# A written-out issue order replaced by another one, with separate PSUM tiles for four early transposes and four of the last stores moved to ScalarE's queue

## The chip, the cores and the metric

The kernel runs on one NeuronCore of one Trainium2 chip. The core has five engines with instruction streams of their own: TensorE (PE in the profile; its weight loads are listed apart as PEld), VectorE (DVE), ScalarE (ACT), GpSimd (POOL, nearly unused here) and SyncE (SP), which here issues nearly all DMA transfers. The engines wait for one another through semaphores only. The metric is device time in microseconds (us); three runs of the kernel before the change took 268.01, 268.32 and 269.27 us, median 268.32 us.

## The reference

Two branches work on a layer-normed input `xn` of 2048 rows and 640 columns, and their sum is added to the raw input.

```python
xn = _layernorm(x, axis=-1)
return x + _A_ref(xn, A_k, A_v, ...) + _B_ref(xn, B_w_gate, B_w_up, B_w_down)

def _A_ref(q, k, v, shift_k, ssm_k, ssm_D):
    k_shift = k_shift + k_pad[:, t:t + S, :] * shift_k[:, ks - 1 - t][None, None, :]   # 4 taps
    kv = k_shift * v
    y = ...                       # long convolution of kv with ssm_k, by FFT of length 2 S
    return q * (y + kv * ssm_D[None, None, :])

def _B_ref(x, w_gate, w_up, w_down):
    h = _sigmoid(g) * u           # g = x @ w_gate, u = x @ w_up, 640 -> 1728
    return h @ w_down             # 1728 -> 640
```

Inputs and output are bf16, S is 2048, D is 640.

## The kernel before, in words

**Branch B** takes the 2048 rows in four row tiles (`tr`) of 512. A row tile is normalized, transposed into `xnT` (for `tr` 0 and 1 by TensorE against an identity, L707; for 2 and 3 by a transposing DMA, L701), multiplied with gate and up weights for 14 column blocks `fc` of 128 (L773: five matmuls of 128x512 to a group; for the first two blocks of `tr` 0 in four column quarters, L753), passed through a sigmoid on ScalarE (L727, L732, L738) and a product on VectorE (L729, L735, L740) into `hT`, and multiplied with `w_down` (L789: groups of 7 or 14 matmuls of 128x320). VectorE adds the result to `acc` (L801), which began as the raw input and ends as the output.

**Branch A** replaces the FFT by two rounds of small DFT matmuls over ten channel slices `idx`. For a slice, VectorE builds `kvt` (L472 to L490); stage 1 (L510) is two groups of 32 matmuls on a quarter of the array's rows; stage 2 (L530) is four groups of 32 matmuls of 64x64; VectorE multiplies the spectra (L554 to L569), which for most slices needs a copy with swapped halves that SyncE issues as two transfers (`P<-S`, L550); stage 3 (L582) is two groups of eight matmuls. After five slices, half the channels are complete, and stage 4 (L614) runs over them: 16 groups in the whole kernel, each of 64 matmuls on 32x32 tiles of the array. ScalarE, and VectorE for the numbers in `ON_DVE`, move each group's result from PSUM to SBUF (L316, L317, L319).

**What orders the work.** Each step calls `plan.op`, which gives it a number and records what it reads and writes. `ORDER` is a written-out permutation of the 984 numbers, and `emit` issues the steps in exactly that order; each engine gets its own steps as a stream and runs them in that order. A planner's due times (`pri`) and costs stand in the source, but the order no longer depends on them. `emit` also hands out buffers: of the free slots of a tag, an unused one, else the one that was used longest ago. PSUM has three slots of tag `c` (2x512 f32 to a partition) and two of tag `g` (512 f32).

The first transposes (`rec_tp` with `fast`) share `psT` tiles, two transposes in one tile of tag `c`; the seven and twelve matmuls that only warm up TensorE (L819) write a tile of tag `g`. The last stores (L632) are 24 DMA issues, all on SyncE's queue.

Of the kernel before, what the change touches and what calls it, by code (L numbers as in the profile page):

```python
# [42 lines left out]
def _dft_tables():  # L43
# [34 lines left out]


ORDER = [  # L80
    1, 0, 4, 5, 42, 6, 7, 8, 71, 12, 13, 11, 72, 10, 73, 74, 75, 91, 96, 86, 87, 76, 77, 78, 14, 2, 104, 16, 81, 625,
    79, 80, 92, 98, 97, 148, 15, 626, 43, 88, 82, 83, 643, 84, 99, 85, 17, 64, 20, 93, 607, 89, 90, 94, 100, 149, 102,
    645, 101, 644, 150, 103, 627, 629, 631, 633, 628, 632, 630, 603, 634, 605, 599, 601, 604, 61, 62, 63, 600, 606,
    602, 18, 639, 641, 650, 640, 651, 153, 152, 652, 108, 642, 635, 608, 609, 23, 637, 611, 66, 106, 67, 151, 610,
    636, 612, 155, 65, 154, 68, 19, 638, 107, 156, 58, 56, 105, 613, 44, 615, 614, 616, 57, 60, 59, 25, 157, 617, 115,
    158, 109, 646, 619, 648, 24, 618, 116, 621, 620, 647, 113, 623, 111, 622, 110, 112, 649, 120, 675, 27, 26, 624,
    122, 3, 679, 676, 117, 121, 119, 118, 123, 130, 678, 680, 22, 683, 21, 661, 124, 114, 673, 29, 662, 665, 674, 663,
    677, 133, 135, 653, 654, 664, 134, 128, 28, 159, 136, 161, 45, 666, 667, 129, 30, 125, 655, 668, 656, 126, 671,
    669, 659, 670, 660, 31, 32, 33, 35, 681, 672, 657, 34, 38, 658, 162, 682, 163, 712, 165, 181, 36, 684, 164, 166,
    37, 127, 714, 713, 703, 182, 715, 704, 705, 39, 685, 167, 168, 172, 160, 706, 298, 687, 689, 47, 171, 169, 691,  # L90
    686, 51, 302, 688, 694, 170, 131, 40, 696, 178, 180, 300, 690, 303, 692, 179, 41, 173, 695, 304, 301, 716, 183,
    195, 697, 299, 718, 196, 174, 730, 199, 49, 200, 175, 693, 201, 732, 202, 197, 176, 717, 186, 69, 177, 95, 719,
    198, 731, 185, 733, 184, 192, 720, 194, 707, 193, 698, 709, 187, 772, 53, 132, 227, 228, 189, 700, 708, 54, 233,
    231, 188, 710, 234, 721, 711, 190, 699, 191, 52, 50, 723, 138, 48, 722, 701, 743, 724, 70, 218, 55, 702, 232, 734,
    139, 744, 137, 203, 736, 213, 229, 725, 745, 46, 214, 140, 735, 727, 205, 207, 204, 206, 141, 209, 737, 230, 208,
    726, 728, 216, 210, 217, 739, 738, 219, 729, 220, 741, 143, 211, 740, 771, 212, 221, 215, 767, 742, 222, 142, 224,
    226, 223, 768, 792, 770, 252, 225, 761, 254, 285, 253, 263, 287, 144, 755, 746, 235, 237, 762, 756, 764, 264, 286,
    269, 255, 758, 270, 265, 256, 267, 239, 236, 266, 791, 241, 786, 238, 240, 257, 268, 242, 249, 773, 288, 788, 753,
    251, 775, 407, 243, 260, 261, 759, 250, 754, 245, 244, 757, 760, 146, 246, 258, 763, 289, 765, 259, 247, 766, 769,
    262, 271, 248, 273, 412, 747, 318, 272, 274, 276, 305, 748, 324, 751, 319, 320, 275, 322, 408, 290, 325, 323, 749,  # L100
    787, 750, 315, 321, 291, 145, 294, 279, 789, 277, 278, 292, 293, 280, 752, 306, 774, 297, 326, 797, 307, 327, 776,
    317, 308, 790, 799, 281, 283, 310, 284, 309, 798, 311, 295, 782, 316, 312, 296, 800, 282, 328, 147, 354, 355, 783,
    313, 784, 329, 358, 359, 331, 356, 801, 410, 360, 793, 361, 785, 777, 345, 340, 330, 314, 795, 344, 779, 414, 778,
    342, 780, 794, 343, 796, 341, 357, 781, 806, 811, 808, 334, 351, 411, 812, 332, 353, 807, 826, 335, 809, 333, 802,
    828, 352, 346, 810, 362, 348, 804, 404, 363, 803, 336, 827, 347, 349, 805, 350, 406, 365, 405, 338, 337, 829, 830,
    817, 831, 339, 926, 413, 822, 819, 424, 383, 824, 364, 367, 427, 832, 927, 418, 426, 425, 834, 818, 833, 428, 366,
    368, 369, 370, 429, 928, 820, 821, 433, 417, 430, 431, 836, 835, 371, 838, 374, 416, 432, 837, 434, 372, 454, 823,
    375, 409, 376, 463, 419, 825, 373, 377, 420, 839, 435, 840, 378, 813, 464, 379, 866, 380, 815, 384, 415, 385, 421,
    387, 814, 449, 386, 422, 423, 450, 816, 848, 850, 381, 452, 460, 851, 451, 436, 438, 388, 461, 382, 462, 437, 849,
    853, 852, 389, 453, 455, 467, 468, 469, 439, 470, 440, 841, 465, 466, 862, 441, 854, 443, 444, 390, 391, 392, 394,  # L110
    457, 863, 865, 442, 397, 398, 399, 400, 855, 456, 867, 844, 471, 401, 858, 445, 845, 458, 856, 446, 490, 459, 488,
    393, 847, 447, 448, 472, 474, 857, 485, 859, 499, 487, 877, 842, 486, 879, 476, 496, 489, 881, 479, 491, 395, 497,
    498, 843, 501, 492, 500, 493, 846, 503, 480, 505, 504, 473, 475, 477, 478, 860, 483, 883, 878, 880, 861, 502, 506,
    481, 872, 507, 484, 521, 864, 482, 494, 527, 402, 874, 523, 495, 528, 873, 882, 508, 875, 907, 509, 511, 522, 531,
    884, 532, 533, 529, 513, 510, 868, 929, 906, 512, 885, 876, 530, 870, 515, 534, 524, 931, 869, 525, 514, 517, 516,
    871, 535, 536, 930, 519, 518, 571, 933, 520, 887, 932, 921, 526, 549, 934, 550, 935, 537, 912, 551, 538, 923, 539,
    914, 541, 886, 553, 552, 555, 540, 585, 542, 554, 543, 922, 544, 924, 556, 913, 915, 925, 916, 557, 558, 917, 919,
    545, 546, 888, 918, 547, 890, 920, 889, 592, 891, 560, 562, 565, 897, 899, 901, 898, 903, 902, 559, 900, 561, 892,
    563, 566, 564, 904, 908, 905, 569, 548, 567, 894, 570, 578, 910, 893, 895, 909, 568, 586, 587, 896, 936, 589, 588,
    911, 396, 590, 591, 967, 579, 580, 582, 581, 938, 572, 573, 583, 939, 584, 575, 593, 574, 941, 576, 594, 937, 595,  # L120
    964, 577, 962, 963, 944, 960, 596, 940, 597, 942, 945, 598, 943, 947, 946, 403, 968, 9, 948, 969, 971, 950, 966,
    949, 952, 951, 970, 961, 953, 974, 972, 973, 965, 954, 975, 955, 958, 978, 977, 979, 976, 956, 957, 959, 982, 980,
    983, 981
]
ON_DVE = [
    101, 103, 135, 134, 136, 656, 660, 526, 915, 546, 548, 570, 895, 588, 581
]


# [90 lines left out]
def kernel(  # L220
# [71 lines left out]
    def make(b, tag, i):  # L292
        shape, dt = SHAPE[tag]
        if b.startswith("pst"):
            shape, dt = [P, NC, P], BF16
        if b.startswith("psT"):
            shape, dt = [P, 2, 1024], BF16
        if b == "wv":
            shape, dt = [P, 4, NC, 512], BF16
        if b in ("xk", "xv"):  # L300
            shape, dt = [P, 2, 2, 4 * DM // 2], BF16
        pool = ps if tag in ("c", "g") else wk
        return pool.tile(shape, dt, name=f"{tag}{i}", tag=f"{tag}{i}")
# [324 lines left out]
    def store(m0, m1, pri, d0=0, d1=DM):  # L628
        key = [("acc", m, x) for m in range(m0, m1) for x in range(4)] if d1 - d0 == DM else (
            [("fin", m, d0 // 320) for m in range(m0, m1)] + [("cv", m // 4) for m in range(m0, m1)])  # L630
        for q in range(4):
            dma(lambda e, q=q: e.dma_start(oq4[q][:, m0:m1, d0:d1], acc[32 * q:32 * q + 32, m0:m1, d0:d1]), 32,  # L632
                2 * (d1 - d0) * (m1 - m0), r=key, w=[("out", m0, d0, q)], pri=pri)

    MEAN, VAR, RST, TMP, EPS = range(5)

# [60 lines left out]
    def rec_tp(tr, pri, fast=False):  # L697
# [8 lines left out]
            for c5 in range(NC):  # L706
                nc.tensor.transpose(o[:, c5, :], tl[N][:, i, c5 * P:(c5 + 1) * P], ident[:])  # L707
        for i in range(4):
            p_ = f"pst{tr}_{i}" if not fast else f"psT{tr}_{i // 2}"
            o = (lambda p_=p_: tl[p_]) if not fast else (  # L710
                lambda p_=p_, i=i: tl[p_][:, i % 2, 0:NC * P].rearrange("p (c n) -> p c n", n=P))
            al = [] if fast and i % 2 else [(p_, "c" if fast else "g")]
            pe(5 * mm(128), 5, lambda i=i, o=o: tp(i, o()), r=[(N, i), ("ident",)] + ([(X, "a")] if i else []),
               w=[(p_, i)] + ([] if i else [(X, "a")]), alloc=al + ([] if i else [(X, "xnT")]), pri=FIX if fast else gt())
            ev(640, lambda i=i: tl[X][:, :, i * P:(i + 1) * P], lambda o=o: o(),
               r=[(p_, i)], w=[(X, i)], pri=pri if fast else pri - 1000)
# [99 lines left out]

    def warm(n):
        for _ in range(n):
            nc.tensor.matmul(tl["wps"][:], lhsT=tl["warm"][:, 0:P], rhs=tl["warm"][:], start=True, stop=True)  # L819
    plan.op({"PE": (4.4, lambda: warm(12))}, r=[("warm",)], w=[("wps", 0)], alloc=[("wps", "g")], pri=FIX)  # L820
    for q in range(2):
        load_x(q, 0, 1, "SP", FIX)
        load_x(q + 2, 0, 1, "ACT", FIX)
# [107 lines left out]
```

## Time and profile before

| what | value |
|---|---|
| median of the runs | 268.32 us |
| time of the profiled execution | 267.2 us |
| span, first to last instruction, of that execution | 265.4 us |
| time around the span | 1.8 us |
| mean granted TensorE clock | 0.983 |
| matmuls, weight loads | 4231, 4231 |
| DVE idle in 78 to 160 us, in 160 to 200 us, in 200 to 236 us | 2.2, 8.2, 5.2 us |

The page lists, for each group of instructions, its line, engine and shapes, its count, the time it was busy, the mean of one, and after the bar the idle time of the engine just before these instructions and what ended it ("issue" where no wait shows). The chain of waits follows the end of the program back to what released each step; a row there has start, duration, engine, tile and line.

### The profile page before, as it was taken

Reading aid. Unit: us, or ns where it says so; the run is one execution under the profiler, and the core shown is the slowest. Engines: PE = TensorE matmul, PEld = TensorE weight load, DVE = VectorE, ACT = ScalarE, POOL = GpSimd, SP = SyncE. Lnnn points to the kernel's source line nnn. Section 1 sums busy time; section 2 is a strip of 40 time slices with the busy share of each in tenths; the row PEclk is TensorE's granted clock in tenths of the full one; section 3 lists DMA queues with packets and bytes.
Section 4 is the critical chain, followed back from the end, with each engine's and each line's share of the span. In section 5 each row is a group of like instructions: output and inputs, shape, how many; then the busy total and the mean of one; then the engine's idle time right before and its main releaser. Section 6 shows DMA issues by size and latency. Waiting matters only on the chain.

```text
span 265.4 us, 9461 instructions
## 1 busy us (share of the span) xinstructions
PE 243.8 (92%) x4231; PEld 145.9 (55%) x4231; DVE 201.2 (76%) x336; ACT 177.2 (67%) x261; POOL 0.7 (0%) x6
## 2 busy tenths in 40 slices
PE   7699999899999999999999994997999899996792
PEld 3554546574455567675645562675675465454571
DVE  4522425568999999999999994896989697996640
ACT  3614699885888998967999993652799774332400
POOL 1000000000000000000000000000000000000000
PEclk9999999999999999999999998897999999999998
DMA  6999979999797199999997953663006496202652
GB/s 175 327 278 244 272 176 132 147 169 149 166 233 207 27 294 183 114 133 135 192 241 194 204 119 94 103 201 82 4 2 180 129 307 158 66 2 54 151 127 73
DMA packets 91024, 41.44 MB, mean 156 GB/s; under 512 B 66656, under 2 KB 88104, under 8 KB 90664
## 3 DMA queue, kind: packets, MB, share of 16 engines
q1 hardware_dynamic: 90792, 40.52, 70.4%
q8 instruction: 33, 0.54, 0.9%
q10 hardware_dynamic: 192, 0.33, 0.4%
q14 instruction: 7, 0.06, 0.1%
HBM read 30.61 MB, written 5.24 MB: 135 GB/s over the span
## 4 chain that ended last, share of the span: by engine, by line
PE 66%; DVE 18%; ACT 6%; issue 6%; DMA 1%; ACTq 0%; DVEq 0%
PE g L773 34%; PE g L789 15%; PE c L530 6%; PE c L614 4%; DVE P L560 3%; PE c L582 3%; ACT jk L654 2%; DVE kvt L490 2%; ACT jk L648 2%; DVE ta L477 2%; PE c L510 2%; DVE acc L801 2%; DVE S L563 1%; PE c L753 1%; DMA acc<-in_A_q_dram 1%
## 5 line engine op out<-in xcount | busy, mean ns | idle before, releaser
L773 PE MATMUL g<-xnT,w 128*128 128x512 bf16 x380 | 90.8, 383 | 0.2 <-DVE acc L801 0.2
L789 PE MATMUL g<-wd,hT 128*128 128x320 bf16 x448 | 68.0, 304 | 0.2
L773 PEld LDWEIGHTS <-w 128*128 128x128 bf16 x380 | 35.0, 98 | 38.1 <-issue 1.7
L789 PEld LDWEIGHTS <-hT 128*128 128x128 bf16 x448 | 42.8, 99 | 18.3 <-issue 0.3
L316 ACT CAST S<-c 128x1024 bf16<-128x1024 f32 x40 | 40.0, 1029 | 6.8 <-PE c L530 6.7
L740 DVE TENSOR_TENSOR hT<-sig,g 128x512 bf16<-128x512 bf16 x32 | 22.0, 686 | 26.7 <-PE g L773 25.6
L738 ACT ACTIVATE sig<-g 128x512 bf16<-128x512 f32 x32 | 19.3, 602 | 22.5 <-PE g L773 19.4
L773 PE MATMUL g<-xnT,V 128*128 128x512 bf16 x140 | 32.7, 379 | 0.1
L801 DVE TENSOR_TENSOR acc<-g,acc 128x320 bf16<-128x320 f32 x32 | 15.5, 488 | 17.8 <-PE g L789 17.7
L530 PEld LDWEIGHTS <-Mt 64*128 64x128 f16 x1280 | 20.0, 95 | 8.3 <-issue 8.0
L530 PE MATMUL c<-T,Mt 64*128 64x64 bf16 x1280 | 22.7, 190 | 1.8 <-issue 1.8
L319 ACT ACTIVATE T<-c 128x1024 bf16<-128x1024 f32 x20 | 20.2, 1028 | 2.1 <-PE c L510 2.1
L490 DVE TENSOR_TENSOR kvt<-ta,vt 128x1024 bf16<-128x1024 bf16 x10 | 21.4, 2144 | 0.1
L773 PEld LDWEIGHTS <-V 128*128 128x128 bf16 x140 | 13.2, 98 | 15.1 <-issue 0.4
L316 ACT CAST V<-c 128x1024 bf16<-128x1024 f32 x17 | 17.3, 1021 | 5.2 <-PE c L582 5.0
L316 ACT CAST T<-c 128x1024 bf16<-128x1024 f32 x19 | 18.9, 1029 | 1.4 <-PE c L510 1.4
L614 PE MATMUL c<-V,Bt 32*32 32x80 bf16 x1024 | 10.8, 204 | 9.6 <-issue 9.6
L614 PEld LDWEIGHTS <-Bt 32*32 32x32 f16 x1024 | 8.8, 88 | 12.9 <-issue 12.0
L477 DVE TENSOR_TENSOR ta<-ta,tb 128x1024 bf16<-128x1024 bf16 x20 | 13.7, 686 | 0.3
L563 DVE TENSOR_TENSOR S<-S 128x1024 bf16<-128x1024 bf16 x20 | 13.7, 687 | 0.3
L732 ACT ACTIVATE sig<-g 128x512 bf16<-128x512 f32 x18 | 10.9, 611 | 4.3 <-PE g L773 2.4
L472 DVE TENSOR_TENSOR tb<-kt,sT 128x1024 bf16<-128x1024 bf16 x20 | 13.7, 684 | 0.0
(87 smaller groups left out, 248.1 us busy)
## 6 DMA issues: line engine op xcount, KB each, us to landing
w<-in_B_w_gate_dram SPq DMA_DIRECT2D x7, 640.0 KB, 4.7
w<-in_B_w_up_dram SPq DMA_DIRECT2D x7, 640.0 KB, 5.9
P<-S SPq DMA_DIRECT2D x14, 256.0 KB, 4.0
kt<-in_A_k_dram SPq DMA_DIRECT2D x8, 320.0 KB, 5.5
vt<-in_A_v_dram SPq DMA_DIRECT2D x8, 320.0 KB, 6.8
xnd<-xq SPq DMA_DIRECT2D x4, 640.0 KB, 5.2
ht<-in_A_ssm_k_dram SPq DMA_DIRECT2D x16, 96.0 KB, 5.2
wd<-in_B_w_down_dram SPq DMA_DIRECT2D x3, 480.0 KB, 9.5
```

Of the source, the lines that this page charges most:

```text
L316: fa = lambda: nc.scalar.copy(out=out_fn(), in_=in_fn())
L319: fa = lambda: nc.scalar.activation(out_fn(), in_fn(), ACT.Copy, scale=scale)
L477: dve(1024, 2, lambda: nc.vector.tensor_tensor(tl[a][:], tl[a][:], tl[c][:] if c != o else tl[c].rearrange("p b n j -> p n b j"), ALU.add) ...
L490: dve(1024, 1 if kt else 2, lambda: nc.vector.tensor_tensor(by_j(tl[o]) if kt else tl[o][:], tl[a].rearrange(form), sl(tl[vb], 0).rearrang ...
L530: nc.tensor.matmul(tl[c][:, b, 64 * kk:64 * kk + 64], lhsT=Mb[rows, k, 64 - 64 * r:192 - 64 * r], rhs=tl[T][rows, 2 * k + r].rearrange("p ...
L563: dve(n, 2, lambda b=b: nc.vector.tensor_tensor(X(b), X(b), H(b), ALU.mult), r=[(Z, b, 0)] + sr, w=[(S_, "p", b)], pri=pri + 0.01)
L614: nc.tensor.matmul(tl[cs[g // 2]][32 * q:32 * q + 32, g % 2, 80 * i:80 * i + 80], lhsT=Bb[32 * g:32 * g + 32, n2, r, :], rhs=tl[V][32 * g: ...
L738: act(512, lambda: nc.scalar.activation(tl[sg][:], pv(0), ACT.Sigmoid), r=[pk(0)], w=[(sg,)], alloc=[(sg, "sig")], pri=pri - 2000)
L740: dve(512, 1, lambda: nc.vector.tensor_tensor(hT[:, fc, :], tl[sg][:], pv(1), ALU.mult), r=[pk(1), (sg,)], w=[(hk, fc)], pri=pri - 2000)
L773: nc.tensor.matmul(tl[c][:], lhsT=w()[:, k, o:o + P], rhs=tl[X][:, k, :], start=(k == 0), stop=(k == NC - 1))
L789: nc.tensor.matmul(tl[pd[i]][:, 0:320], lhsT=hT[:, fc, t4 * P:(t4 + 1) * P], rhs=wd[:, fc, 320 * i:320 * i + 320], start=(fc == 0), stop=( ...
L801: dve(320, 1, lambda i=i, m=m, pd=pd: nc.vector.tensor_tensor(acc[:, m, 320 * i:320 * i + 320], tl[pd[i]][:, 0:320], acc[:, m, 320 * i:320 ...
```

## The change

`ORDER` is replaced as a whole (984 numbers before and after, the same steps). On TensorE the same 4231 matmuls are issued in another order. The 16 groups of stage 4 stood in eight pieces of two groups (128 matmuls); they now stand in six pieces of two groups and four of one, with other groups between them. `ON_DVE` changes by a few numbers (16 steps in place of 15). In the ORDER, the one early `Sqrt` on a constant (step 9) moves from the end of ScalarE's stream to its first steps. The order of the loads and stores on SyncE changes with the rest.

The first transposes get one `pst` tile each (tag `g`), and the warming matmuls a tile of tag `c`. Of the last eight stores (`m0 == 15`), the four with odd `q` are issued by ScalarE.

```diff
 ORDER = [
-    1, 0, 4, 5, 42, 6, 7, 8, 71, 12, 13, 11, 72, 10, 73, 74, 75, 91, 96, 86, 87, 76, 77, 78, 14, 2, 104, 16, 81, 625,
...
+    2, 0, 5, 4, 6, 8, 7, 10, 71, 72, 12, 73, 1, 11, 13, 14, 42, 74, 75, 91, 96, 76, 77, 78, 16, 81, 86, 79, 80, 92,
...
 ON_DVE = [
-    101, 103, 135, 134, 136, 656, 660, 526, 915, 546, 548, 570, 895, 588, 581
+    101, 103, 133, 134, 135, 136, 656, 658, 884, 875, 525, 518, 915, 570, 581, 575
 ]
...
-        if b.startswith("psT"):
-            shape, dt = [P, 2, 1024], BF16
...
-                2 * (d1 - d0) * (m1 - m0), r=key, w=[("out", m0, d0, q)], pri=pri)
+                2 * (d1 - d0) * (m1 - m0), q="ACT" if m0 == 15 and q % 2 else "SP", r=key, w=[("out", m0, d0, q)], pri=pri)
...
-            p_ = f"pst{tr}_{i}" if not fast else f"psT{tr}_{i // 2}"
-            o = (lambda p_=p_: tl[p_]) if not fast else (
-                lambda p_=p_, i=i: tl[p_][:, i % 2, 0:NC * P].rearrange("p (c n) -> p c n", n=P))
-            al = [] if fast and i % 2 else [(p_, "c" if fast else "g")]
+            p_ = f"pst{tr}_{i}"
+            o = lambda p_=p_: tl[p_]
+            al = [(p_, "g")]
...
-            nc.tensor.matmul(tl["wps"][:], lhsT=tl["warm"][:, 0:P], rhs=tl["warm"][:], start=True, stop=True)
-    plan.op({"PE": (4.4, lambda: warm(12))}, r=[("warm",)], w=[("wps", 0)], alloc=[("wps", "g")], pri=FIX)
+            nc.tensor.matmul(tl["wps"][:, 0], lhsT=tl["warm"][:, 0:P], rhs=tl["warm"][:], start=True, stop=True)
+    plan.op({"PE": (4.4, lambda: warm(12))}, r=[("warm",)], w=[("wps", 0)], alloc=[("wps", "c")], pri=FIX)
```

In TensorE's stream of the second half of stage 4, a piece of 128 matmuls was followed by 7 matmuls of L789 and the next piece of 128, four pieces in all. After the change it reads (matmuls by the line of the kernel before): 128 of L614, 10 of L773, 128 of L614, 5 of L773, 64 of L614, 14 of L789, 64 of L614, 14 of L789, 128 of L614.

## Prediction

> **What bounds the kernel now.** I read the page's shares first, then the chain of waits by time, then TensorE's rows in the list of groups. TensorE is busy for 92% of the span and VectorE for 76%:
>
> ```profile
> PE 243.8 (92%) x4231; PEld 145.9 (55%) x4231; DVE 201.2 (76%) x336; ACT 177.2 (67%) x261; POOL 0.7 (0%) x6
> ...
> q8 instruction: 33, 0.54, 0.9%
> ...
> PE 66%; DVE 18%; ACT 6%; issue 6%; DMA 1%; ACTq 0%; DVEq 0%
> ...
> L530 PE MATMUL c<-T,Mt 64*128 64x64 bf16 x1280 | 22.7, 190 | 1.8 <-issue 1.8
> ...
> L614 PE MATMUL c<-V,Bt 32*32 32x80 bf16 x1024 | 10.8, 204 | 9.6 <-issue 9.6
> ```
>
> TensorE waits for almost no other engine; 11.4 us of its idle time (9.6 in L614, 1.8 in L530) are "issue": nothing the profile shows held it. The chain shows where (start, duration, what):
>
> ```profile
> 159.66 0.46 PE c L614 x44
> 160.11 3.78 issue
> 163.89 0.89 PE c L614 x84
> 164.78 2.24 PE g L773 x5
> ...
> 176.45 0.40 issue
> ...
> 179.16 1.42 issue
> 180.57 0.51 PE c L614 x43
> 181.09 3.43 PE g L789 x14
> ```
>
> ```profile
> 238.32 1.42 issue
> 239.74 0.76 PE c L614 x72
> 240.50 1.06 PE g L789 x7
> 241.55 0.50 PE c L614 x49
> 242.05 1.14 issue
> 243.19 0.82 PE c L614 x79
> ```
>
> The waits fall inside uniform pieces, so no data is missing. Count what runs between two of them: 72 + 7 + 49 = 128 matmuls with 128 weight loads, 256 instructions. The page's instruction queue moved 0.54 MB for 8462 TensorE instructions, 64 bytes each, in 33 packets of 16.4 KB: 256 instructions a packet. All seven waits of 0.4 us and more stand, to within three instructions, at the same place modulo 256 in TensorE's stream. So TensorE waits for its next packet of instructions. I call the stretch between two such places a block.
>
> Its turnaround can be read as well. From resuming to resuming in the same chain takes 243.19 - 239.74 = 3.45 us, and 3.7 us for two other blocks (176.85 to 180.57, 243.19 to 246.92). In the trace's records of that queue the packet starts 1.1 us after a block is entered, takes 0.9 to 1.3, and TensorE resumes 1.3 to 1.5 later. A block with under about 3.6 us of its own work must wait. Twice it was slower: at 161.41 and 204.18 the packet started 3.7 and 3.1 us after the block was entered, just as other transfers ran out (the DMA engines were 0.95 busy in 157.3 to 160.2), and those blocks lasted 6.2 and 6.1 us.
>
> A second cost hangs on the first (busy time of PE, PEld, DVE, ACT, POOL; then granted clock):
>
> ```profile
> 164.80:167.10 2.30, 2.30 (x17) 0.64 (x21) 0.00 (x0) 1.29 (x2) 0.00 (x0) 0.50 0.03 7
> ...
> 181.10:184.60 3.50, 3.50 (x17) 2.13 (x18) 1.91 (x4) 1.29 (x2) 0.00 (x0) 0.56 0.65 153
> ```
>
> After two of the waits the clock was granted at half for 3.4 us each. L773 x5 took 2.24 us instead of 1.08, L789 x14 3.43 instead of 1.90; with the smaller groups beside them (L789, L510, L582) 3.4 us in all.
>
> **The new order, step by step.** The same matmuls are issued, so only waits can go. *1. Instruction packets.* I cut the new stream into blocks of 256 at the same place and priced each from the chain: 1.16 us for 128 matmuls of L614, 0.57 for 32 of L530, 0.34 for 32 of L510, 0.45 for 8 of L582, 1.08 for 5 of L773, 0.95 for 7 of L789. Before, five blocks held 2.05 to 2.20 us of work and one 3.05. In the new order the block with 40 of L614, 10 of L773 and 78 of L614 holds 0.36 + 2.17 + 0.71 = 3.24, and none holds less. Six hold under 3.6: 3.40, 3.35 (first half of stage 4), 3.27 (mostly L530), 3.24, 3.34, 3.58 (second half). With 3.6 us as turnaround they wait 0.2 + 0.25 + 0.33 + 0.36 + 0.26 + 0.02 = 1.4 us; with 3.45 it is 0.7, with 3.73 2.2. The first two stand beside a `P<-S` swap and two or three 640 KB weight loads, where a late packet is likely: I add one at 6.2 - 3.6 = 2.6 us. Left over: 4.0 of 11.4, a gain of **7.4** (10.7 with 0.7 left and no late packet; the other end is under "Slower").
>
> *2. Half clock.* In the second half of stage 4 the same 1.1 to 1.4 us waits cost no clock, with one L789 group between pieces; at 160 and 179 the waits were longer or less full work stood beside them. With 5 to 10 long matmuls between pieces and shorter waits I expect nearly all 3.4 back: **3.0** (none if a 3 us wait falls among L614 again).
>
> *3. Head.* L753 waits twice for a copy out of a shared transpose tile: at 8.53 for 0.78 us (ScalarE copied the first transpose at 8.57, though it was done at 6.03) and at 12.84 for 0.58 (VectorE copied at 12.88 both transposes of a pair). With own tiles the second goes; the first is then held by the two weight halves issued at 2.79 and 3.23, whose landing takes 5.7 and 5.8 us, so until 9.0. **0.7**, between 0 and 0.9. The weights that follow are asked for in another order; with 9.6 MB queued before the last `w_down` piece in both orders, that piece lands near 39.7 as before and is needed a little under 42.
>
> *4. Middle.* At 49.53 TensorE idles 0.84 us for a normalization on ScalarE (L687), behind 12 statistics. The new order has it on VectorE and fewer statistics ahead: **0.8** (0 to 0.84).
>
> *5. End.* VectorE's last add ends at 260.79, but SyncE issues eight stores at 0.46 us each from 259.64 and starts the last at 262.85; it lands 1.5 later. With two of the last four on ScalarE, idle by then, the last can start near 261.3; the table load and `Sqrt` that leave the end of ScalarE's stream were hidden anyway. **1.4** (0.5 to 1.9).
>
> *6. What is late next.* VectorE is idle for 2.2 us of 82 between 78 and 160 us, and for 13.4 of 76 between 160 and 236 us, where TensorE wants back 3.78 + 0.40 + 1.42 + 1.56 of waits and 3.4 of clock, 10.6 in all. It fits with under 3 us to spare, and VectorE's own order differs: adding up both engines' durations in each order from the L740 at 77.57, with no other waits, VectorE comes up to 2.0 us late for TensorE before and 2.6 after. I charge **1.5** (0 to 5). SyncE queues the last up-weight load behind the last swap; from the earliest issue to its first use TensorE has some 3 to 4.8 us of work, while such loads land in 4.2 us at best and 5.9 in the median. **1.0** (0 to 2.9).
>
> *Sum.* 7.4 + 3.0 + 0.7 + 0.8 + 1.4 - 1.5 - 1.0 = 10.8 us. The profiled execution took 267.2 (span 265.4 and 1.8 around it), 1.1 under the median, so it would take 256.4, and the median of runs **257.5 us**.
>
> One rule speaks against the largest term. The Trainium skill, "Runtime: NRT & Kernel Launch", section "Instruction fetch mechanics", gives TensorE room for 2048 instructions refilled in pieces of 256, and calls the crossing "mostly hidden". The trace agrees on the 256 and not on the hiding: the stretch from 236 to 248 us holds under 1200 instructions and waited three times. By that rule terms 1 and 2 would vanish, and the sum would be some 2.9 us without term 6.
>
> **Rivals.** *Late packets.* For: the two blocks of 6.1 and 6.2 us. Against: the waits from 238 on, when the DMA engines were 0.13 busy. If three more blocks in the first half of stage 4 are late as well, the other one of the two above (2.6) and two that hold 3.86 and 3.88 us (2.3 each), less the 0.2 already charged, that is 7.0 more: 264.5. *VectorE becomes the bound.* For: its 97% between 78 and 160. Against: the idle time after 160. If half of the 10.6 us is lost to it: 262. *The order does not do what it says:* the waits have another cause and stay, and only terms 3 to 5 act: 265.5. *Slower.* All eight blocks under 4 us last 6.2: 8 x 6.2 - 27.9 = 21.7 us of waits instead of 11.4, with the half clock kept and terms 3 to 5 gained: 268.3 + 10.3 - 2.9 = 275.7. It decides from about 1.8 us more per block than the quiet 3.6, that is, if transfers fill the DMA engines at each of these places; before, they did so at two.
>
> **How the numbers follow.** Forecast 257.5, which covers 253.5 to 260.5, chance 0.72; late packets 0.10; VectorE 0.10; no effect of the order 0.04; slower 0.04. The range 253.5 to 264.5 takes in the first three but for their outer ends. A measurement of this kernel tells about 0.5% from no change, 1.3 us: faster 0.93, same 0.03, slower 0.04.
>
> **What would show it.** Right: L614's "issue" idle under 4 us and no 1.4 us wait in the second half of stage 4; a granted clock of 0.99 or more between 160 and 200; no idle before L753 from a copy; the last store under 1 us after VectorE's last add. Wrong: "issue" waits of 2.5 us at 256-instruction distance where `P<-S` and weight loads run; TensorE waiting for VectorE (L801, L740) between 160 and 200, or for a weight load near the end of L773.

## The result, and the profile after

Four runs of the new kernel took 262.01, 257.57, 259.05 and 258.6 us, median **258.83 us**; the kernel before, beside them, 268.16 us. The ratio is 0.9649 (95% interval 0.9558 to 0.974). Forecast were 257.5 us and a range of 253.5 to 264.5. Medians here are of all runs, while ratios leave out the executions that took over 1.5% longer than the fastest of their kernel (that of 262.01 us among them), so both are given.

The profiled execution is the one of 262.01 us (span 259.9), the slowest of the four; it is read against its own time. In the new kernel's numbering L528, L612, L770, L786 and L750 are the L530, L614, L773, L789 and L753 of before. From its page, shares, the instruction queue, the chain of waits and three groups of TensorE (idle time after the bar):

```profile
PE 244.0 (94%) x4231; PEld 146.1 (56%) x4231; DVE 201.2 (77%) x337; ACT 175.5 (68%) x259; POOL 0.7 (0%) x6
...
q8 instruction: 33, 0.54, 0.9%
...
PE 64%; DMA 18%; DVE 5%; SPq 4%; issue 3%; ACT 3%; DVEq 0%; ACTq 0%
...
L770 PE MATMUL g<-xnT,w 128*128 128x512 bf16 x380 | 90.9, 379 | 2.6 <-ACT sig L735 1.3
L786 PE MATMUL g<-wd,hT 128*128 128x320 bf16 x448 | 68.5, 306 | 2.0 <-issue 2.0
...
L528 PE MATMUL c<-T,Mt 64*128 64x64 bf16 x1280 | 22.8, 191 | 2.2 <-issue 2.2
```

TensorE's busy time is what it was (243.8). Its waits for nothing the profile shows ("issue") stand in L528 and L786 now, 4.2 us where 11.4 had been. In the chain of waits "issue" has 3% for 6%; DMA has 18% for 1%, because the chain now runs through loads of the input (11 to 33 us) and two weight loads (138 and 216 us). Behind its first matmul TensorE idles 6.7 us in gaps over 0.15 us instead of 14.9, and its last matmul ends at 252.17 instead of 260.26. The span fell by 5.5 us only: between TensorE's last matmul and the end lie 7.7 us, where 5.1 had been.

The two places that the forecast showed, the first in the chain of waits of the new kernel (start, duration, what), the second in TensorE's time line (idle time before the group in brackets):

```profile
156.70 2.27 PE g L770 x10
158.97 0.62 PE c L612 x64
159.59 0.25 PE c L528 x9
159.84 1.85 issue
161.69 0.51 PE c L528 x23
...
165.21 0.69 issue
165.89 3.65 PE g L786 x13
```

```profile
230.25 1.23 PE L612 MATMUL c<-V,Bt 32*32 32x80 bf16 x128
231.41 1.25 PE L770 MATMUL g<-xnT,w 128*128 128x512 bf16 x5
232.59 0.93 PE L612 MATMUL c<-V,Bt 32*32 32x80 bf16 x64
234.81 2.06 PE L786 MATMUL g<-wd,hT 128*128 128x320 bf16 x14 [1.28 <-issue]
```

Of 3.78, 0.40 and 1.42 us between 160 and 181 are left 1.85 and 0.69, of three waits behind 236 one of 1.28. But L786 x13 took 3.65 us at 165.89, at the price of the other groups 1.8: half clock again, for 6.8 us in a row (in windows of the trace: length, busy PE, PEld, DVE, ACT, POOL, then granted clock, DMA share, GB/s):

```profile
163.30:166.70 3.40, 2.71 (x42) 1.29 (x40) 2.42 (x2) 2.38 (x4) 0.00 (x0) 0.50 1.08 181
166.70:170.15 3.45, 3.45 (x37) 2.01 (x37) 0.57 (x2) 0.69 (x2) 0.00 (x0) 0.50 1.08 272
```

The end, from the time lines of VectorE, ScalarE's queue and SyncE's queue (start, duration from first to last of the group, what):

```profile
251.78 1.75 ACTq L630 DMA_DIRECT2D out_dram<-acc  x4
252.21 0.49 DVE L798 TENSOR_TENSOR acc<-g,acc 128x320 bf16<-128x320 f32 x1 [0.46 <-PE g L786]
```

```profile
253.29 4.51 SPq L630 DMA_DIRECT2D out_dram<-acc  x10
```

and from the list of waits, what SyncE's queue waited for (us in total, times, longest):

```profile
SPq L630 <- DMA out_dram<-acc: 5.3, 2, 3.2
```

VectorE's last add ends at 252.70, ScalarE has issued its four stores by 253.5, and SyncE issues ten more, one after the other, until 257.8. They were not held by data: SyncE stood at the first of them (row block 14) from 249.99 to 253.24, waiting for a transfer of another store.

### The profile page after: what moved, and what is told of

Same layout as the page of the kernel before. It is cut to its first block, busy times and chain, and to the rows that moved or that the text cites. A ratio compares the mean times of both kernels' runs of the same rounds, so it can differ in the third digit from the quotient of the medians.

```text
span 259.9 us, 9463 instructions
## 1 busy us (share of the span) xinstructions
PE 244.0 (94%) x4231; PEld 146.1 (56%) x4231; DVE 201.2 (77%) x337; ACT 175.5 (68%) x259; POOL 0.7 (0%) x6
## 4 chain that ended last, share of the span: by engine, by line
PE 64%; DMA 18%; DVE 5%; SPq 4%; issue 3%; ACT 3%; DVEq 0%; ACTq 0%
PE g L786 25%; PE g L770 25%; DMA acc<-in_A_q_dram 9%; PE c L528 6%; DMA w<-in_B_w_up_dram 5%; DMA vt<-in_A_v_dram 3%; PE c L612 3%; PE c L580 3%; PE c L508 2%; DMA P<-S 2%; ACT S L314 1%; SPq L378 1%; SPq L352 1%; DVE hT L737 1%; SPq L827 1%
## 5 line engine op out<-in xcount | busy, mean ns | idle before, releaser
L770 PE MATMUL g<-xnT,w 128*128 128x512 bf16 x380 | 90.9, 379 | 2.6 <-ACT sig L735 1.3
L786 PE MATMUL g<-wd,hT 128*128 128x320 bf16 x448 | 68.5, 306 | 2.0 <-issue 2.0
L770 PEld LDWEIGHTS <-w 128*128 128x128 bf16 x380 | 34.7, 98 | 41.1 <-issue 2.6
L786 PEld LDWEIGHTS <-hT 128*128 128x128 bf16 x448 | 42.6, 99 | 19.4 <-issue 2.3
L314 ACT CAST S<-c 128x1024 bf16<-128x1024 f32 x40 | 39.4, 1026 | 8.1 <-PE c L528 8.0
L770 PE MATMUL g<-xnT,V 128*128 128x512 bf16 x140 | 32.8, 379 | 0.0
L528 PEld LDWEIGHTS <-Mt 64*128 64x128 f16 x1280 | 20.2, 96 | 8.7 <-issue 8.1
L528 PE MATMUL c<-T,Mt 64*128 64x64 bf16 x1280 | 22.8, 191 | 2.2 <-issue 2.2
L770 PEld LDWEIGHTS <-V 128*128 128x128 bf16 x140 | 13.3, 98 | 15.7 <-DMA V<-in_B_w_up_dram 0.5
L314 ACT CAST V<-c 128x1024 bf16<-128x1024 f32 x18 | 18.2, 1026 | 3.2 <-PE c L580 3.1
L729 ACT ACTIVATE sig<-g 128x512 bf16<-128x512 f32 x18 | 10.8, 602 | 5.0 <-PE g L770 3.3
L567 DVE TENSOR_TENSOR S<-P 64x1024 bf16<-64x1024 bf16 x18 | 12.4, 689 | 0.6
L565 DVE TENSOR_TENSOR S<-S 64x1024 bf16<-64x1024 bf16 x18 | 12.4, 687 | 0.6
```

The costliest lines, as they stand in the source:

```text
L314: fa = lambda: nc.scalar.copy(out=out_fn(), in_=in_fn())
L528: nc.tensor.matmul(tl[c][:, b, 64 * kk:64 * kk + 64], lhsT=Mb[rows, k, 64 - 64 * r:192 - 64 * r], rhs=tl[T][rows, 2 * k + r].rearrange("p ...
L770: nc.tensor.matmul(tl[c][:], lhsT=w()[:, k, o:o + P], rhs=tl[X][:, k, :], start=(k == 0), stop=(k == NC - 1))
L786: nc.tensor.matmul(tl[pd[i]][:, 0:320], lhsT=hT[:, fc, t4 * P:(t4 + 1) * P], rhs=wd[:, fc, 320 * i:320 * i + 320], start=(fc == 0), stop=( ...
```

## The experiments

My theory after the result: the packets of instructions explain what TensorE won (A); the end was lost to a semaphore that the two queues share (B); the waits of 1.9 us and more that are left come from packets that start late because bulk transfers fill the DMA engines (C). Rivals: the waits belong to the data or tiles of these groups; the end is bound by SyncE's 0.46 us a store; a packet takes what it takes.

**The changed kernel again.**

> The changed kernel unchanged, five more runs. If the half clock (6.8 us of it between 163 and 170 in the profiled execution of 262.01 us) is what set that execution above the other three (257.6 to 259.1), a faster execution has one window of 3.4 us or none there and L786 x13 takes some 2 us instead of 3.65; time 257.5 to 259. If instead the windows belong to every execution of this order, the granted clock between 160 and 200 stays near 0.91 and something else (a later transfer) differs.

Median 259.7 us of six, ratio 0.9661 (0.9602 to 0.972). In its profile (259.49 us) the half clock lasts 3.4 us, from 162.7 to 166.1, behind a packet wait of 2.12 us at 159.40. The L786 group in question falls into the end of it and takes 2.63 us (14 matmuls from 165.05), between the two expected values. With one window less this execution took 2.5 us less. Two versions below with TensorE's order unchanged (24 stores on SyncE, 12 on ScalarE) show no half clock there at all, so the windows do not belong to the order as such. The end is the same: SyncE waits until 250.72, 7.7 us from TensorE's end to the span's end.

**B. The stores.** In the compiled program each transfer is given one of eight completion semaphores in turn (in the traces of the end: 100, 102, 103, 104, 106, 107, 108, 109), over both queues together, and an instruction that takes one first waits until the transfer before it on that semaphore has landed. In the trace ScalarE's four stores hold semaphores 104, 106, 107 and 108; SyncE's next store takes 104. It waits on 104 until 253.24, 1.5 us after ScalarE issued its store on 104 at 251.78.

```diff
-... q="ACT" if m0 == 15 and q % 2 else "SP", r=key, ...
+... q="SP", r=key, ...
```

> The changed kernel with all 24 stores on SyncE again, order kept. Theory (a completion semaphore shared by the two queues): SyncE waited from 249.99 to 253.24 for a store that ScalarE could issue only at 251.78, with 14 stores behind it; without ScalarE's stores that wait goes, SyncE issues 18 stores from 250.0 at 0.46 us and starts the last near 256.4 to 257 at the latest, so it is 0.5 to 1.5 us faster than the changed kernel, although SyncE has four stores more. Rival (the end is bound by SyncE's 0.46 us a store and nothing else): four stores more make it 1.8 us slower.

Median 256.36 us, ratio 0.9563 (0.9506 to 0.962): 3.3 us under the changed kernel by the medians (2.6 by the ratios), with four stores *more* on SyncE. Its queue now runs through (time line of SyncE):

```profile
246.23 6.42 SPq L629 DMA_DIRECT2D out_dram<-acc  x14
```

The last 14 stores start at 246.23 and are out at 252.65 (I had counted 18 from 250.0); TensorE ends at 249.48, and 5.3 us lie from there to the span's end, 2.4 less than in the changed kernel: this part is the stores'. The rest of the 3.3 may be the clock's, as this profile shows no half clock before TensorE's end. The rival (1.8 us slower) is out.

```diff
-... q="ACT" if m0 == 15 and q % 2 else "SP", r=key, ...
+... q="ACT" if m0 in (12, 14) or m0 == 15 and q % 2 else "SP", r=key, ...
```

> The changed kernel with the stores of row blocks 12 to 13 and 14 on ScalarE as well, 12 of 24. Semaphore theory: no store of SyncE then reuses the semaphore of a ScalarE store that is issued later than about 249.5, so SyncE's last store starts within 1.5 us of VectorE's last add and the end comes 4 to 4.5 us after TensorE's end instead of 7.7: 2.5 to 3.5 us faster than the changed kernel, near 255.5. Rival (ScalarE's stores wait for the same adds and the transfers themselves take the time): within 0.7 us of the changed kernel.

Median **255.19 us**, ratio 0.9503 (0.9449 to 0.9556), the lowest median of the study; its interval overlaps that of the version before it. Both queues end within 1.2 us of each other (time lines of the two queues and VectorE):

```profile
248.87 1.88 ACTq L629 DMA_DIRECT2D out_dram<-acc  x4
248.88 3.02 SPq L629 DMA_DIRECT2D out_dram<-acc  x5
249.29 0.49 DVE L797 TENSOR_TENSOR acc<-g,acc 128x320 bf16<-128x320 f32 x1 [0.46 <-PE g L785]
```

SyncE's last store starts at 251.58, 1.8 us behind VectorE's last add (1.5 expected at most); from TensorE's end to the span's end it is 4.8 us, 0.5 less than with all stores on SyncE. The rival (within 0.7 us of the changed kernel) is out. SyncE still waits for semaphores (8.8 us in its list), but for stores that were issued earlier.

The same edit of the change, alone, in the kernel before:

```diff
-... (m1 - m0), r=key, ...
+... (m1 - m0), q="ACT" if m0 == 15 and q % 2 else "SP", r=key, ...
```

> The kernel before with only the q argument: the four odd stores of the last row block on ScalarE. The forecast's step 5: the last store starts 1.4 us earlier (0.5 to 1.9), the time falls by as much. Semaphore theory from the changed kernel: SyncE's store of row block 14 that comes eight transfers behind ScalarE's first one waits for it, so SyncE stands until 1.5 us after that store was issued and then issues six to eight more; no gain, between 0 and 1.5 us slower.

Median 269.54 against 267.97 us, ratio 1.0162 (1.0087 to 1.0238): slower. SyncE waits until 257.76 for the store that ScalarE issued at 256.31, and 6.7 us instead of 5.1 lie behind TensorE's end, a loss of 1.6 us, as by the medians; the ratio says more than the end explains. Theory B holds; the forecast's step 5 is wrong by itself, in either order.

**The head.** The kernel before with own tiles only (with the warming matmuls' tile in the other pool, as in the change):

```diff
-            p_ = f"pst{tr}_{i}" if not fast else f"psT{tr}_{i // 2}"
...
-            al = [] if fast and i % 2 else [(p_, "c" if fast else "g")]
+            p_ = f"pst{tr}_{i}"
+            o = lambda p_=p_: tl[p_]
+            al = [(p_, "g")]
```

> The kernel before with only the first transposes' own PSUM tiles (and the warm-up's tile in the other pool). By the forecast's step 3: TensorE no longer idles 0.58 us at 12.84 and waits for weights instead of ScalarE's copy at 8.53, so the head gains 0.7 us (0 to 0.9) and the time falls by as much, since TensorE is on the path everywhere behind. Rival, from the profile of the changed kernel, whose stream had come 2.1 us further by 12.2: the gain is 1.5 to 2.1 us. Second rival: a later wait for a weight half or the statistics (0.8 to 1.3 us between 33 and 50) takes it back and the time stays within 0.3 us.

Median 265.53 against 267.19 us, ratio 0.9951 (0.9905 to 0.9996). TensorE's early rows:

```profile
8.62 1.28 PE L752 MATMUL c<-xnT,V 128*128 128x128 bf16 x20
...
10.28 1.28 PE L752 MATMUL c<-xnT,V 128*128 128x128 bf16 x20
...
11.68 1.28 PE L752 MATMUL c<-xnT,V 128*128 128x128 bf16 x20
```

No copy holds L752 (L753 of before), nor do weights: it starts at 8.62, not at 9.0. The 0.41 us ahead of a transpose at 10.59 went too, and the third group starts at 11.68 instead of 13.43, 1.75 us earlier. The first rival's size (1.5 to 2.1) is right for the head; in time the medians say 1.7 us, the ratio 0.1 to 2.5.

**A. The packets.** First, 128 instructions more at the head: 32 small matmuls in `warm`, which is called twice, so 64 matmuls and 64 weight loads. (The expectation counted one call; the theory then asks for 64 matmuls, half of a block, instead of 32.)

```diff
+        for _ in range(32):
+            nc.tensor.matmul(tl["wps"][:, 0:64], lhsT=tl["warm"][:, 0:P], rhs=tl["warm"][:, 0:64], start=True, stop=True)
```

> The kernel before with 32 matmuls of 64 columns (64 instructions) more in the warm-up. Packet theory: every wait keeps its place modulo 256 in TensorE's stream, so in the code all of them move 32 matmuls earlier: the one that came after 44 matmuls of an L614 piece comes after 12, those after 72 and 49 come after 40 and 17. Rival (the waits belong to these instructions, their data or their tiles): they stay after 44, 72 and 49. Time by both: up to 2 us longer for the warm-up, nothing else expected.

Half a block earlier is half a block later than the next block's place, so the waits behind 44, 56, 49 and 42 matmuls of an L614 piece should stand behind 108, 120, 113 and 106. The chain:

```profile
165.51 0.99 PE c L614 x108
166.50 2.40 issue
...
239.51 1.09 PE c L614 x120
240.60 1.32 issue
...
243.21 1.03 PE c L614 x113
244.24 1.14 issue
...
246.69 0.97 PE c L614 x106
247.66 1.17 issue
```

To the matmul. (Between 176 and 185 us one wait of 1.97, at 182.56, stands where there were two of 0.40 and 1.42. All seven waits of 0.4 us and more, two of them at places that had none, stand at the same place modulo 256 in TensorE's stream, to within one instruction.) The same instructions, with the same data and tiles, now run without a wait where they waited before. (Median 269.97 us, ratio 1.0162, 1.0073 to 1.0251: the first L753 starts 1.7 us later.) The rival is out.

Then the order alone, in the second half of stage 4 of the kernel before (TensorE's steps; VectorE's adds for them go along):

```diff
-586, 587, 936, 579, 580, 938, 572, 573, 939, 593, 594, 937, 944, 942, 945, 943
+586, 587, 936, 937, 938, 579, 580, 939, 942, 943, 572, 573, 944, 945, 593, 594
```

> The kernel before with the new idea in the second half of stage 4 only: between the four L614 pieces stand 21, 21 and 21 matmuls of L789 instead of 7, 7 and 7. Packet theory: each stretch of 128 matmuls there then holds 3.2 to 3.8 us of work instead of 2.2, so the three waits of 1.42, 1.14 and 1.42 us shrink to 0.6 us or less in sum: 3.4 to 4.0 us faster, less what VectorE's later adds take at the end (0 to 1). Rival (the waits have another cause than the distance between packets): they stay in the L614 pieces and the time stays within 0.5 us.

```profile
240.39 2.96 PE g L789 x21
243.34 1.16 PE c L614 x128
244.50 2.01 PE g L789 x14
246.51 1.16 PE c L614 x128
...
248.72 1.05 issue
```

The three stretches hold 21, 21 and 14 matmuls (not 21 each, as the expectation says). Three waits (3.98 us) became one of 1.05, behind the pieces, and one of 0.29 for VectorE. TensorE ended at 256.60 instead of 260.26, 3.7 us earlier, with half clock in the same two windows as before. The span fell by 1.9 only: SyncE now issues stores without a pause from 251.44 to 261.36, and 6.9 us lie behind TensorE's end. Median 265.83 against 267.97 us, but the ratio is 1.0034 (0.9989 to 1.008), which tells no gain. What the order does to TensorE is shown; what it is worth by itself is not.

**C. Late packets.** One weight load of 640 KB moved ahead of the swap, in the kernel before:

```diff
-435, 840, 378, 813, 464, 379, 866, 380
+866, 435, 840, 378, 813, 464, 379, 380
```

> The kernel before with one 640 KB weight load moved in SyncE's queue from between the two halves of the swap P<-S at 155 us to ahead of both, where it can be issued near 151. Theory (the packet of the 6.2 us block was late because that load and the two halves filled the DMA engines from 156.4 to 161.2): the DMA engines are free of them 2.3 us earlier, the packet starts near 159 instead of 161.4, and the wait of 3.78 us at 160.11 shrinks to 1.2 to 1.8; the half clock behind it (1.2 us) may go too. The packet asked for at 152 may be late instead (0 to 0.8). In all 1.5 to 3.5 us faster. Rival (a packet takes what it takes, whatever else moves): the wait stays at 3.5 us or more and the time within 0.5 us.

The load did not go near 151: SyncE waited for TensorE to free its buffer and issued it at 155.03, only 0.9 us earlier than before, and the swap behind it was issued by 156.80 instead of 157.28. The packet started at 160.31 instead of 161.41, and the wait fell from 3.78 to 2.47 us: half of what was expected, from an edit that moved the transfers far less than expected, so that it tests theory C only in direction. Half clock followed all the same, and the wait at 177.68 grew from 1.42 to 2.21 us while the one of 0.40 went. Median 266.13 against 267.97 us, ratio 1.0037 (0.9996 to 1.0078): no gain that can be told.

In the changed kernel, three loads (886, 926, 927) moved behind the place; SyncE's steps:

```diff
-436, 866, 886, 926, 927, 390, 841, 867, 928, 397, 471, 472
+436, 866, 390, 841, 867, 926, 927, 928, 397, 471, 472, 886
```

> The changed kernel with three weight loads (640, 240 and 160 KB) moved in SyncE's queue: the two smaller ones behind the next up-weight load, near 168 us, the large one behind the swap that is issued at 176 to 178; all three are needed after 184. Theory (the packet asked for near 156.5 starts only at 159.0 to 159.3 because these loads and a swap fill the DMA engines from 154 to 161): the packet starts by 157.5, TensorE's wait of 1.9 to 2.2 us at 159 to 160 shrinks to 0.5 or less, and the half clock behind it, seen in two of three profiled executions of this order with the late packet, is not there: 1.5 to 2 us faster than the changed kernel, up to 3.5 against an execution with half clock. Rival (a packet simply takes over 5 us there): the wait stays near 2 us and the time within 0.5 us. Second rival: the moved loads make a later packet (171 or 180 us) late instead, and the gain is given back there.

```profile
158.35 1.48 issue
...
181.12 1.08 PE g L769 x5
182.20 0.34 PE c L579 x6
182.54 1.06 issue
```

The packet started at 157.55 instead of 159.05 to 159.29, yet TensorE still waited 1.48 us; and the one asked for near 179 was late, beside the load put there (DMA engines 0.90 busy from 176 to 180), after another wait of 0.96 us at 173.54: the second rival. Median 261.31 us against 266.95 for the kernel before, beside it; the ratio, 0.9812 (0.9746 to 0.9878), is worse than the changed kernel's 0.9661. With 12 stores on ScalarE as well:

> The same three moved loads, and 12 of the 24 stores on ScalarE as in the version with row blocks 12 and 14 there. If both gains are independent, it ends 4.5 to 5 us after TensorE's end and takes 253 to 254 us, 1 to 2 us under the version with the stores alone (255.2); rival as for the moved loads alone: 255 to 255.5.

257.5 us, ratio 0.9676 (0.961 to 0.9742), 2.3 us above the version with the stores alone (0.9503), with waits of 2.37 and 1.67 us at the same two places.

Last, in the version with the 12 stores, one load moved ahead of the swap (435, 436), and then both; SyncE's steps:

```diff
-435, 376, 436, 866, 886
+866, 435, 376, 436, 886
```

```diff
-435, 376, 436, 866, 886
+866, 886, 435, 376, 436
```

> The version with row blocks 12 and 14 stored by ScalarE, and one 640 KB weight load moved in SyncE's queue from behind the swap P<-S that is issued at 152 to 154 us to ahead of it, where SyncE stands idle from 144.9 to 152.2 and the DMA engines from 147 to 152.6. Theory (a packet starts late when bulk transfers fill the DMA engines, and the transfers that stay must not meet another packet): the bulk behind the swap runs out near 158 instead of 161, the packet asked for near 157 starts by 158 instead of 159, and the wait of 2.2 us at 159.3 falls to 0.5 to 1.2; no later packet is touched. 1 to 1.7 us faster than that version (255.2), so 253.5 to 254.2. Rival: the packet asked for near 145 to 147 is the late one now, a new wait of 0.5 to 1.5 us near 151 takes the gain back, and the time stays at 255 or above.

> The same, and the second 640 KB weight load ahead of the swap as well; its buffer comes free near 150.3, so it can run from 150.3 to 153.5. Theory: the wait at 159.3 falls to 0 to 0.5 us, but this load now runs where the packet of the block entered at 151 is asked for, which is needed at 155.7: if that packet still starts by 153.5 the time is 253 to 253.8; if it starts only when load and swap have run out (156 to 157), TensorE waits 2 to 3.5 us near 155.7 and the time is 255.5 to 257.5.

258.85 us (ratio 0.9701, 0.9635 to 0.9767) and 260.46 us (0.9758, 0.9704 to 0.9811): both worse. Time line of SyncE's queue in the first:

```profile
141.93 1.21 SPq L691 DMA_DIRECT2D xnd<-xq  x1
153.16 0.37 SPq L377 DMA_DIRECT2D w<-in_B_w_gate_dram  x1
153.70 0.60 SPq L547 DMA_DIRECT2D P<-S  x1
```

The load could not be issued early: it waited for TensorE to free its buffer until 153.16, and the swap behind it went 1.5 us later than without the move. I had taken the buffer for free at 144.9. The packet wait at 158 to 159 stayed (2.43 us; 2.02 in the second version). The next wait has a cause beside packets; the chain of waits in the first version:

```profile
154.97 8.24 DMA P<-S
...
165.34 0.61 DVE hT L736
...
165.99 0.43 PE g L785
166.42 0.67 issue
```

The delayed swap landed at about 163.2, so VectorE started on it at 163.31 (at 158.34 without the move) and was late with the product (L736) that TensorE waits for: 1.32 us here, and 3.29 in the second version, where the product ended at 168.06. The packet of this place was late as well (164.58, 3.6 us behind the block's beginning) and held TensorE for the last 0.67 us in the first. As a test of theory C these two say little; as a move they lose.

## Why the prediction was right, and where it was not

The forecast was 1.3 us under the median of its four runs (the six later ones have 259.7 us against 267.19 beside them, a gain of 7.5 us), but the sum is nearer than its terms. In the profiled execution, where 10.8 us were expected, the time fell by 5.2 (the measured terms make 5.0):

| step | forecast | measured | from |
|---|---|---|---|
| 1 packets | +7.4, 4.0 left | +7.2, 4.2 left | 11.4 less (0.37 + 1.85 + 0.69 + 1.28) |
| 2 half clock | +3.0 | 0 here | 6.8 us at half before and after |
| 3 head | +0.7 | +2.1 | instruction 192 of the stream at 12.19 instead of 14.32 |
| 4 middle | +0.8 | +0.8 | no wait at 49.5 |
| 5 end | +1.4 | -2.6 | 7.7 instead of 5.1 us behind TensorE |
| 6 late next | -2.5 | -2.5 | 1.33 + 0.49 + 0.50 + 0.2 |

**1 was right in mechanism; that the size came out is in part luck.** Blocks of 256, the same turnaround (in the shifted stream 3.46 and 3.45 us from resuming to resuming) and a long late packet between 156 and 160, as charged. But the forecast put the boundaries of the new stream's second half nine matmuls too late. Counted back from the wait at 233.53, its block with "40 of L614, 10 of L773 and 78 of L614" holds 49, 10 and 69; priced at 3.24 us, it was to wait 0.36 and did not wait. The next one, priced at 3.34 with a wait of 0.26, holds 59 of L614, 5 of L773 and 64 of L614, only 2.2 us by the forecast's own prices, and waited 1.28. So "none holds less" is wrong. The two short blocks waited 1.97 us (0.69 + 1.28) where six were to wait 1.4; late packets cost 2.22 (1.85, and 0.37 at 82.8) where 2.6 were charged; the errors cancelled. *Late packets* as a rival needed three more in the first half of stage 4; none came there. *The order does not do what it says* is excluded by the shifted stream. VectorE did not become the bound: TensorE waited for it 0.2 us.

**2 failed in this execution.** The forecast allowed for that only "if a 3 us wait falls among L614 again"; a wait of 1.85 us in L528, behind 64 small matmuls, was enough. Over the runs it came in part: mean clock times span gives a median of 12.8 us at half clock for the kernel before (61 runs) and 7.2 for the new one (10 runs), the time behind the last matmul included. Over the runs of the kernel before, time rises by 0.29 us per us at half clock (correlation 0.89), from which I estimate 1.6 us of the 3.0.

**3 was mis-sized.** "Held by the two weight halves ... until 9.0" took median landing times, longer than these two loads needed, and did not count the waits ahead of the transposes. Own tiles alone brought the third group 1.75 us forward; the rest of the 2.1 came with the new order.

**5 failed.** "With two of the last four on ScalarE ... the last can start near 261.3" treats the two queues as independent. They share completion semaphores, and a store of SyncE came to stand behind a store of ScalarE that was issued later. Without these four stores on ScalarE the stretch behind TensorE's end is 2.4 us shorter and the median 3.3 us lower.

**6 had the right sum from other parts.** The charge for VectorE (1.5) was not needed; weights cost 1.0 as charged, but only half of it at the load that was named (0.50 at 220.49; the 0.49 at 145.45 fell on another). In its place L770 waited 1.33 us at 33.56 for a sigmoid: ScalarE's statistics (L646) stood ahead of it in its stream, for a row block that landed at 33.35. The forecast had looked there for late `w_down` weights only. It was 0.14 to 0.94 us in the seven other profiles of the new kernel and its variants.

The rule that the forecast weighed, the Trainium skill's "Runtime: NRT & Kernel Launch", section "Instruction fetch mechanics", calls the crossing of a block "mostly hidden". The runs agree where blocks hold some 4 us of work and the packet is not late (a late one left a wait of 0.37 us behind 5.3 us of work at 82.8), and not where short blocks follow one another: there 3.7 us of TensorE's time went away by re-ordering four pieces.

**Open.** Why a packet that is asked for under bulk traffic starts 2.2 to 3.8 us after the block's beginning, and not at once: it was neither always last behind the bulk (at 159.3 the bulk ran on until 163) nor always late (145.8). And no moved load removed the wait at 159, so that theory C explains its direction and not its size. Nor is it known why the boundaries of the new stream lay nine matmuls from where the forecast put them.

## What to carry to other kernels

Where a uniform wait shows no cause, count instructions between two of them: a stretch of 256 instructions with less than its packet's turnaround of work (3.45 to 3.7 us here, from wait to wait) is likely to wait, and longer matmuls between the short ones are the cure. One such stretch behind a longer one can pass (3.34 us at 227.46 in the new kernel, 3.12 at 243.34 in the order-only version, both without a wait); two in a row did not. Count the boundaries from a trace of the new stream, since nine matmuls decided over 1 us. Before stores are given to a second queue, look up which completion semaphores its transfers share with the first, and choose them so that no store of the first queue takes the semaphore of one that the second issues later: here the last four alone cost time, and the same four with eight earlier ones did not. A transfer moved away from one packet meets the next one, and a load moved ahead takes its wait for a buffer with it and holds the queue, in one case the swap that VectorE and then TensorE waited for: judge a move by everything it is put in front of.

## What the runs showed of the hardware

**The clock is decided in windows of 3.41 us.** All changes of the granted clock in an execution lie on one grid of 3.413 us whose phase differs between executions. The kernel before, in two such windows and the one behind each:

```profile
160.96:164.37 3.41, 0.48 (x63) 0.46 (x62) 1.65 (x1) 0.00 (x0) 0.00 (x0) 1.00 0.07 13
164.37:167.79 3.42, 3.42 (x84) 1.48 (x71) 0.66 (x2) 1.47 (x3) 0.00 (x0) 0.51 0.02 5
178.03:181.45 3.42, 2.00 (x135) 1.43 (x133) 2.50 (x5) 0.39 (x2) 0.00 (x0) 1.00 0.07 17
181.45:184.86 3.41, 3.41 (x19) 2.15 (x17) 2.17 (x4) 0.97 (x2) 0.00 (x0) 0.51 0.60 144
```

Over the 14 profiles, counted from 20 us on, a window at full clock in which TensorE was busy for less than 0.49 of it was followed by half clock 11 times of 11; between 0.49 and 0.7, 7 times of 35; above, in none of over 850. So the wait of 1.42 us at 179.16 (its window 0.58 busy) brought half clock and the one at 238.32 (0.65) did not, and where the grid falls is a part of the spread of the runs. The Trainium skill, "TensorE: Matmul & The Clock Gate", section "HAM oscillation — how this bites in real kernels", states the rule as no idle gap above some 3.4 us; here waits of 1.1 to 3.8 us were enough (1.14 at 177.77 with own tiles only), where the small matmuls around them leave a window's busy share under 0.7, so the measurement is the stricter one.

**A second queue can slow the first.** The skill's "DMA: Bandwidth & Descriptors", section "Issuing engines are not separate DMA queues", expects of a second issuing engine only the saved issue time. Here it cost 2.4 us behind TensorE's end (3.3 by the medians) with the four last stores, and gained 0.5 there (1.2 by the medians, within the spread) with twelve.
